# A long convolution with a soft mixture of experts: the filter's first stage kept on chip, and four moves at the end of the kernel

## The chip, the cores and the metric

The kernel runs on one core of one Trainium2 chip, everything in float32. The metric is the device time of one execution in microseconds (us). Lower is better.

## The reference, cut to what matters

```python
# x (8, 5696, 128), h (5696, 128), phi (128, 32), w1 (8, 128, 1024), w2 (8, 1024, 128)
Yf = rfft(x, n=2 * S, axis=1) * rfft(h, n=2 * S, axis=0)[None]
t = irfft(Yf, n=2 * S, axis=1)[:, :S].reshape(8 * S, 128)      # 45568 tokens
logits = t @ phi                                               # 32 slots, 4 for each of 8 experts
d = softmax of logits over the tokens (per slot)
slot_input = d.T @ t                                           # (32, 128)
slot_out[e] = relu(slot_input[e] @ w1[e]) @ w2[e]
c = softmax of logits over the slots (per token)
out = c @ slot_out                                             # (45568, 128)
```

A causal convolution of each batch with one filter h comes first. Every token then gives its logits, and all tokens together give 32 slots. The output of a token is a mixture of the 32 results, so no output can be written before the last token is through.

## The kernel before, in words

The sequence of 5696 tokens is taken as 89 rows by 64 columns, and the transform of length 5760 (N1 = 90 by N2 = 64) as matrix products in stages A, B and C. The columns are folded: column n with column 63 - n, as a sum (`comp` 0) and a difference (`comp` 1), which leaves 32 columns for each. A chunk is four columns and their four mirrors, so a batch has eight chunks. The filter h goes through the same front as the batches, as batch number 0 of nine; the 72 chunks are numbered on through them.

- Stage A. `load_x` (L178) loads a chunk. `fold` (L195) forms sum or difference on GpSimd (L200). `stage_a` (L204) multiplies the table `s1` (128x128, stationary) with 512 elements of tokens (L211), twice; ScalarE copies the two results to a tile `fst` of three buffers (L213), and two DMAs store it to `f` in DRAM (L217). TensorE handles float32 in more than one pass, so a matmul has two records in the trace.
- Stage B works on units: 23 a batch, each two of 45 rows. `load_g` (L224) loads one from `f` into a tile `gt`. `stage_b1` (L235) multiplies it (L244) in tiles of 64x64. For a batch, VectorE forms the products with the filter's spectrum, pr (L265), pi (L268) and their sum yf (L270). For the filter itself (`g == 0`), ScalarE makes `ph` (L253), VectorE from it the tiles `Hr` (L255) and `Hi` (L258), for two halves, and GpSimd the negative of Hi (L261). `stage_b2` (L274) transforms yf back (L284), ScalarE copies the result to `zst` (L288), and a DMA stores it to `z` in DRAM.
- Stage C works on pairs of chunks, 32 in all. `load_pair` (L308) loads one from `z`; c1 (L324) is the last product and the unfolding, with additions on VectorE and GpSimd (L360); c2 (L366) transposes the tokens into `yt`; c3 (L376) gives the logits `lt`; `column_max` (L386) keeps a running maximum per slot; c4 (L404) transposes the logits and takes their exponential for the dispatch; c5 (L428) transposes that one; `softmax` (L437) is the one over slots: an exponential on ScalarE (L439), the sum rs (L441), an addition (L442) and a reciprocal (L443) on VectorE, a product on GpSimd (L444); `dispatch` (L448) adds to the slots' inputs (L455, L460); c6 (L475) transposes the combine weights (L479), which go to `c_t` in DRAM, and `load_c`, `place` and `place_all` (L499, copies at L501) bring them back into the tile `cT` in the tail.

The order is written out by hand; no planner moves anything. A loop over t (L558) runs from 0 to 80. Step t holds stage A of chunk t (up to t=71), three units of stage B lagging by nine steps (LAG_B), and parts of stage C of up to six pairs lagging by 27 and more (LAG_C), interleaved by `slot_b`. From t=72 there is no stage A any more and `without_a` (L594) gives the order: even in its pairs, the steps with a c1 call `softmax` right after c5 and the additions, and the steps between hold dispatch, c2, c6, c3 and `column_max`. The last front below means these steps, t=71 to 80.

After the loop comes the tail: the last batch's pairs without stage B (from L683), `join_quarters`, the experts' two layers (hid at L801 to L812, its transposes at L819, the second layer at L827), and the slots' results `so` and `so4` (L831, L836). The output loop (from L854) multiplies 32x128 of `cT` (stationary, read in order) with `so4` (L863) into four banks per tile of up to four windows of 8 rows, copies them out on VectorE (L870) and ScalarE (L872), and stores them (L874): there every partition holds runs of four neighbouring tokens, 2 KB in DRAM.

All DMAs are issued on SyncE's queue (SP), in the order of the code, but some constants on ScalarE's. Each DMA waits until the one eight before it on its queue has landed, for its semaphore.

Of the kernel before, what the change touches and what calls it, by code (L numbers as in the profile page):

```python
# [22 lines left out]
def transform_tables(S, N1, N2, CH, X0, F0, F1):  # L23
# [11 lines left out]

    N, R1, HALF, P = N1 * N2, S // N2, N2 // 2, 2 * N2
# [8 lines left out]
    part = s1  # L45
    s1 = np.zeros((P, 3, P))
# [24 lines left out]
    return [np.ascontiguousarray(t, dtype=np.float32) for t in (s1, i1, wq, vq, tn)]  # L71
# [3 lines left out]
def kernel(  # L75
# [8 lines left out]
):  # L84

# [36 lines left out]
    t_s1, t_i1, t_w, t_v, t_turn = [  # L122
        nc.inline_tensor(t, f"tab_{n}").ap()
        for n, t in zip(("s1", "i1", "w", "v", "turn"), transform_tables(S, N1, N2, CH, X0, F0, F1))]
    fd = [nc.dram_tensor(f"f_{g}", (2, N2, NP, 2, D), F32, kind="Internal").ap() for g in range(B + 1)]
# [52 lines left out]
    def load_x(c):  # L178
# [3 lines left out]
        src = (h if g == 0 else x[g - 1]).rearrange("(a n) d -> a n d", n=N2)  # L182
# [21 lines left out]
    def stage_a(c, comp):  # L204
# [11 lines left out]
        for a, p in enumerate((F0, F1)):  # L216
            nc.sync.dma_start(  # L217
                out=fd[g][a, n0:n0 + CH, :, :, :].rearrange("n q c d -> q n (c d)"),
                in_=st[p:p + NP, :, :, :].rearrange("k n c d -> k n (c d)"))


    gs, prods = {}, {}

    def load_g(u):  # L224
        if u >= (B + 1) * NU:
# [6 lines left out]
            in_=fd[g].rearrange("a r q c d -> (a r) (q c d)")[:, 4 * i * D:(4 * i + 2 * n) * D])  # L232
        gs[u] = t_

    def stage_b1(u, adder=nc.vector):  # L235
        g, i = divmod(u, NU)
        n = min(2, NP - 2 * i)
        t_ = gs.pop(u)
# [35 lines left out]
    def stage_b2(u):  # L274
# [12 lines left out]
        st = bpool.tile([P, 2, 2 * D], F32, name="zst", tag="zst", bufs=5)  # L287
# [8 lines left out]
    ybufs = [ypool.tile([P, Q * CH, D + 1], F32, name=f"y{i}") for i in range(2)]  # L296
# [5 lines left out]
    nc.vector.memset(zring[0][:, :, :, :, :, :], 0.0)  # L302
    for t_ in (lt, dt):
        nc.vector.memset(t_[:, :, :, :], 0.0)
    for t_ in ybufs:
        nc.vector.memset(t_[:, :, D:D + 1], 1.0)
# [225 lines left out]

    def units(t):
        g, i = divmod(t - LAG_B, NJ)
        if t < LAG_B or g > B:
            return []
# [3 lines left out]
    queue = [(u, t) for t in range(steps) for u in units(t)]  # L540
# [4 lines left out]
    load_x(0)  # L545
    nc.scalar.dma_start(out=s1[:, :, :], in_=t_s1)
    for c in range(1, 3):
        load_x(c)
# [5 lines left out]
    for comp in range(2):  # L554
        fold(0, comp)
    wait_b2 = []

    for t in range(last_front + 1):  # L558
# [13 lines left out]
        def slot_b():  # L572
            fresh = bool(us)
            if fresh:
# [3 lines left out]
                wait_b2.append(u)  # L578
            if len(wait_b2) > fresh:
# [14 lines left out]
        def without_a():  # L594
# [7 lines left out]
            if T is not None:  # L602
# [10 lines left out]
                softmax(U)  # L613
# [6 lines left out]
            assert t < last_front or not (us or wait_b2)  # L620
            if t == last_front:
# [5 lines left out]
        if t == NA:  # L627
# [284 lines left out]
```

## Time and profile before

| | us |
|---|---|
| median of 3 runs | 928.26 (925.73 to 928.39) |
| profiled execution | 923.57 |
| its span in the profile | 921.4 |
| TensorE busy (PE) | 832.2, 90% of the span, 7220 instructions |
| VectorE busy (DVE) | 658.7, 71% |
| ScalarE busy (ACT) | 512.9, 56% |
| GpSimd busy (POOL) | 472.9, 51% |
| DMA | 273.04 MB, 296 GB/s on the mean |

The profile comes from one execution, whose time stands beside its span. A group line has the line of the code, the engine, the operation, the program's names of what it writes and reads, the partitions and elements, and the count; after the bar, busy time in us and mean ns of one, and after the next bar the idle time of the engine just ahead of these instructions and what ended it. A timeline line begins with its start and its duration in us; what stands in brackets at its end is the idle time before it and what ended that. A windows line gives, for a stretch of time, the busy us and the instructions of each engine, the granted TensorE clock (1.00 is full), the busy share of the DMA engines and the GB/s they moved.

The order of time is this: t=0 starts at 7.9 us, t=8 at 40.4, t=10 at 57.9, t=12 at 70.7, t=17 at 104.1, t=28 at about 200, t=71 at 681.8; the c1 steps of the last front follow each other at 19.8 us on the mean (687.6 to 786.7); the output loop runs from 855.7 to 921.4.

### The profile page before, as it was taken

The page shows a single profiled execution, that of the slowest core. Times are in us where ns is not written, and L with a number is a line of the kernel's source. Part 1 is how long each engine was busy: PE and PEld are TensorE (multiplying, and loading weights), DVE is VectorE, ACT ScalarE, POOL GpSimd, SP SyncE. Part 2 cuts the span into 40 slices and gives each one's busy share as a digit, 9 for nine tenths or more (in the row PEclk, how much of TensorE's full clock was granted, in tenths as well). Part 3 has the DMA queues.
Part 4 walks back from the last instruction along what each step waited for, and adds up shares of the span by engine and source line. Part 5 has one row for each costly group of instructions (what it writes and reads, how often), then busy time and mean ns, then how long its engine had stood idle before and what let it go on. Part 6 is the DMA issues. An engine that isn't in the chain of part 4 may idle for free. (4 is left out here: it accounts for less than half of the span.)

```text
span 921.4 us, 20366 instructions
## 1 busy us (share of the span) xinstructions
PE 832.2 (90%) x7220; PEld 401.8 (44%) x7220; DVE 658.7 (71%) x1122; ACT 512.9 (56%) x1018; POOL 472.9 (51%) x434
## 2 busy tenths in 40 slices
PE   6968888889999999999999999999997878997894
PEld 2323233334444444444444444444443334454783
DVE  3035677578888887888788888878878888685442
ACT  3546544445666565666666666656664444585442
POOL 4647632345565555555555555555544666574300
PEclk9989999999999999999999999999999998999755
DMA  9989899999999999999999999999998887783998
GB/s 294 277 264 277 268 311 332 299 290 310 307 284 314 287 305 275 324 322 299 307 341 325 290 274 316 318 292 309 312 313 259 290 276 234 256 286 138 339 405 333
DMA packets 172239, 273.04 MB, mean 296 GB/s; under 512 B 14742, under 2 KB 117398, under 8 KB 168965
## 3 DMA queue, kind: packets, MB, share of 16 engines
q1 hardware_dynamic: 171563, 271.38, 92.4%
q8 instruction: 58, 0.95, 0.4%
q10 hardware_dynamic: 576, 0.36, 0.2%
q14 instruction: 42, 0.34, 0.1%
HBM read 142.85 MB, written 128.21 MB: 294 GB/s over the span
## 5 line engine op out<-in xcount | busy, mean ns | idle before, releaser
L211 PE MATMUL bank<-x,s 128*128 128x512 f32 x576 | 284.5, 621 | 9.6 <-POOL x L200 7.9
L200 POOL TENSOR_TENSOR x<-xc 128x512 f32<-128x512 f32 x144 | 183.7, 1276 | 144.3 <-PE bank L211 90.4
L213 ACT ACTIVATE fst<-bank 128x512 f32<-128x512 f32 x288 | 167.9, 597 | 92.5 <-PE bank L211 63.5
L265 DVE TENSOR_TENSOR pr<-bt,Hr 128x512 f32<-128x512 f32 (+1 forms) x184 | 126.6, 688 | 96.7 <-PE bt L244 93.8
L288 ACT ACTIVATE zst<-bz 128x512 f32<-128x512 f32 (+1 forms) x184 | 108.2, 588 | 150.3 <-PE bz L284 140.9
L244 PE MATMUL bt<-gt,wt 64*64 64x256 f32 x1620 | 138.0, 404 | 47.9 <-DMA gt<-f 13.7
L211 PEld LDWEIGHTS bank<-x,s 128*128 128x128 f32 x576 | 100.2, 192 | 133.1 <-issue 89.5
L270 DVE TENSOR_TENSOR yf<-pr,pi 128x512 f32<-128x512 f32 (+1 forms) x169 | 145.8, 863 | 5.8
L268 DVE TENSOR_TENSOR pi<-bt,Hi 128x512 f32<-128x512 f32 (+1 forms) x184 | 125.0, 679 | 0.0
L284 PE MATMUL bz<-yf,vt 64*64 64x256 f32 x1440 | 117.2, 386 | 2.5 <-DVE yf L270 0.8
L244 PEld LDWEIGHTS bt<-gt,wt 64*64 64x64 f32 x1620 | 45.0, 132 | 164.0 <-issue 41.9
L336 PE MATMUL bank<-zc,i 128*64 128x512 f32 x448 | 108.0, 604 | 0.0
L360 POOL TENSOR_TENSOR y<-y,op 128x512 f32<-128x512 f32 x64 | 77.5, 1211 | 59.3 <-DVE op L341 56.8
L360 POOL TENSOR_TENSOR y<-y,om 128x512 f32<-128x512 f32 x59 | 81.8, 1387 | 2.1
L284 PEld LDWEIGHTS bz<-yf,vt 64*64 64x64 f32 x1440 | 52.9, 133 | 37.9 <-issue 12.8
L255 DVE SCALAR_TENSOR_TENSOR Hr<-bt,turn,ph 128x128 f32<-128x128 f32 (+1 forms) x46 | 16.0, 349 | 68.9 <-ACT ph L253 68.9
L372 ACT ACTIVATE yt<-bank 128x360 f32<-128x360 f32 x128 | 51.8, 472 | 17.0 <-PE bank L370 17.0
L370 PE MATMUL bank<-ident,y 109*128 109x109 f32 x512 | 58.1, 266 | 0.9 <-POOL y L360 0.8
L370 PEld LDWEIGHTS bank<-ident,y 109*128 109x128 f32 x512 | 49.8, 143 | 16.0 <-issue 10.8
L416 POOL MEMSET dt<- 64x8 f32 x32 | 3.4, 107 | 100.8 <-ACT dn L419 79.7
L863 PE MATMUL op<-so,cT 32*128 32x128 f32 x704 | 47.3, 398 | 5.4 <-ACT o L872 5.1
L390 DVE TENSOR_REDUCE mx<-lt 64x1 f32<-64x360 f32 x64 | 33.0, 516 | 25.0 <-ACT lt L382 24.6
(100 smaller groups left out, 895.5 us busy)
## 6 DMA issues: line engine op xcount, KB each, us to landing
f<-fst SPq DMA_DIRECT2D x288, 180.0 KB
gt<-f SPq DMA_DIRECT2D x198, 256.0 KB
z<-zst SPq DMA_DIRECT2D x176, 256.0 KB
zc<-z SPq DMA_DIRECT2D x28, 1024.0 KB
xc<-in_x_dram SPq DMA_DIRECT2D x64, 320.0 KB
out_dram<-o SPq DMA_DIRECT2D x15, 1024.0 KB
zc<-z SPq DMA_DIRECT2D x28, 416.0 KB
out_dram<-o SPq DMA_DIRECT2D x9, 768.0 KB
```

The source lines that it names most:

```text
L200: nc.gpsimd.tensor_tensor(out=y_[:, :, :], in0=t_[:, 0, :, :], in1=t_[:, 1, ::-1, :], op=AL.subtract if comp else AL.add)
L211: nc.tensor.matmul(p[:, :], s1[:, tab[G], :], src[:, :, :].rearrange("p n d -> p (n d)"), start=True, stop=True)
L213: nc.scalar.activation(st[:, :, G, :], p[:, :].rearrange("p (n d) -> p n d", d=D), AF.Copy)
L244: nc.tensor.matmul(bt[q * HP:(q + 1) * HP, a, 0:2 * D], wt[r, 2 * i + q, :], t_[r, q, :, :].rearrange("p c d -> p (c d)"), start=True, sto ...
L265: nc.vector.tensor_tensor(out=pr[r, :, :, :], in0=pv, in1=Hr[r, i, :, :].unsqueeze(2).broadcast_to([n * HP, 2, 2, D]), op=AL.mult)
L268: nc.vector.tensor_tensor(out=pi[r, :, :, :], in0=pv, in1=Hi[r, i, :, :, :], op=AL.mult)
L270: adder.tensor_tensor(out=y_[r, :, :, :], in0=pr[r, :, :, :], in1=pi[r, :, ::-1, :], op=AL.add)
L284: nc.tensor.matmul(bz[a * HP:(a + 1) * HP, q, 0:2 * D], vt[r, i, a, :], y_[r, a, :, :].rearrange("p c d -> p (c d)"), start=True, stop=True)
L288: nc.scalar.activation(st[:, 0:n, :], bz[:, 0:n, 0:2 * D], AF.Copy)
L336: nc.tensor.matmul(p[h_ * HP:(h_ + 1) * HP, :], i1[:, tab, :], t_[:, h_, o, :, q, :], start=True, stop=True)
L360: eng.tensor_tensor(out=part(v, f), in0=part(v, 0), in1=o_[:, :, :], op=sign)
L370: nc.tensor.transpose(p[:, i * TR:(i + 1) * TR], ys[T][0:TR, k * CH + i, 0:D], ident[0:TR, 0:TR])
```

## The change

1. The filter's stage A no longer goes through DRAM. `load_h` loads all of h into the space of `Hi` in runs of 8 KB; `fold_h` puts the sum into the space of `Hr` and the difference back in place. `stage_a_of_filter` takes five of the 128 feature columns at a time: the stationary operand is 89 tokens by 32 columns of the folded array for one feature (its neighbours 512 bytes apart), the moving one a new table `sh` of 90 columns, 20 matmuls into the four column tiles of one bank. Four copies put a bank's contents into four tiles that aren't used yet (zc, y, zst, yt), where stage B of the filter reads them. There are 26 such groups.
2. The order at the start. The loop begins at t=12. Before it stands stage A of the first batch's chunks 8 to 11, with seven groups of the filter after each half chunk from chunk 10 on. The filter's 23 units are spread over t=12 to 16 (before: t=9 to 16), up to two in a slot. The tiles lent to the filter are cleared on GpSimd at t=17.
3. Step t=71 has the form of `without_a`, its stage A stands at the end of step 70; in `without_a` the softmax of a pair moves to the following step, behind c2 and ahead of c6, c3 and `column_max`. The loads of the first half of w1 come two steps later.
4. In the tail, one c6 moves behind the c5 of the last chunk but one, and the last c6's move behind the transposes of the experts' hidden layer.
5. The outputs. A tile has 32 rows, 24 in the last. The stationary operand reads `cT` with a stride of four elements for 32 rows, two for 16 and none for 8, so that a partition holds 16, 8 or 4 neighbouring tokens: runs of 8, 4 or 2 KB in DRAM. Matmuls and copies are as many as before.

The diff, cut:

```diff
+    sh = np.stack([s1[:, i:i + 2].reshape(R1, 2, 2, N1 // 2).transpose(0, 2, 1, 3)
+                   for i in range(2)], 1)
...
-        t_ = gs.pop(u)
+        t_ = gs.pop(u) if g else of_filter(2 * i, n)
...
-    nc.vector.memset(zring[0][:, :, :, :, :, :], 0.0)
     for t_ in (lt, dt):
-        nc.vector.memset(t_[:, :, :, :], 0.0)
-    for t_ in ybufs:
-        nc.vector.memset(t_[:, :, D:D + 1], 1.0)
+        nc.gpsimd.memset(t_[:, :, :, :], 0.0)
+
+    def clear():
+        nc.gpsimd.memset(zring[0][:, :, :, :, :, :], 0.0)
+        for t_ in ybufs:
+            nc.gpsimd.memset(t_[:, :, D:D + 1], 1.0)
...
+    def load_h():
+        src = h.rearrange("(a n) d -> a n d", n=N2)
+        k = HALF // 2
+        for n0, gap, run in ((0, N2 - k, k), (k, HALF - k, HALF - k)):
+            for r in (slice(0, SPLIT), slice(SPLIT, R1)):
+                v, o_ = src[r, n0:n0 + run, :], hraw[r, n0:n0 + run, :]
+                v, o_ = [bass.AP(tensor=w.tensor, offset=w.offset,
+                                 ap=[w.ap[0], [gap * D, 2], [1, run * D]]) for w in (v, o_)]
+                nc.sync.dma_start(out=o_, in_=v)
+
+    def fold_h():
+        k = HALF // 2
+        for n0, eng in ((0, nc.gpsimd), (k, nc.vector)):
+            lo = hraw[:, n0:n0 + k, :]
+            up = hraw[:, N2 - 1 - n0:N2 - 1 - n0 - k:-1, :]
+            nc.vector.tensor_tensor(out=hsum[:, n0:n0 + k, :], in0=lo, in1=up, op=AL.add)
+            eng.tensor_tensor(out=lo, in0=lo, in1=up, op=AL.subtract)
+
+    HG = 5
+
+    def stage_a_of_filter(d0):
+        n = min(HG, D - d0)
+        p = bank()
+        for k in range(n):
+            for a in range(2):
+                for comp, t_ in enumerate((hsum, hraw)):
+                    r = a * HP + comp * HALF
+                    nc.tensor.matmul(p[r:r + HALF, k * 2 * NP:(k + 1) * 2 * NP],
+                                     t_[:, 0:HALF, d0 + k], sh[:, comp, a, :],
+                                     start=True, stop=True)
+        pv = p[:, 0:n * 2 * NP].rearrange("p (d c q) -> p q c d", c=2, q=NP)
+        for i, (q0, m, t_) in enumerate(homes):
+            dst, src = t_[:, :, :, d0:d0 + n], pv[:, q0:q0 + m, :, :]
+            if i in (1, 2):
+                nc.vector.tensor_copy(out=dst, in_=src)
+            else:
+                nc.scalar.activation(dst, src, AF.Copy)
...
-    load_x(0)
+    load_x(NJ)
     nc.scalar.dma_start(out=s1[:, :, :], in_=t_s1)
+    load_h()
+    nc.scalar.dma_start(out=sh, in_=t_sh.rearrange("p h a c q -> p h a (c q)"))
...
     for comp in range(2):
-        fold(0, comp)
-    wait_b2 = []
-
-    for t in range(last_front + 1):
+        fold(NJ, comp)
+    fold_h()
+    groups = list(range(0, D, HG))
+    for c in range(NJ, T0):
+        for comp in range(2):
+            stage_a(c, comp)
+            fold(c + 1, comp)
+            for _ in range(7 if c > NJ + 1 else 0):
+                if groups:
+                    stage_a_of_filter(groups.pop(0))
+        load_x(c + 3)
+    wait_b2, due = [], []
+
+    for t in range(T0, last_front + 1):
...
                 stage_b1(u)
                 wait_b2.append(u)
+                if u < NU and us:
+                    stage_b1(us.pop(0))
...
-                softmax(U)
+                due.append(U)
                 return
...
+            if due:
+                softmax(due.pop())
...
+        if t == NA - 2:
+            for comp in range(2):
+                stage_a(t + 1, comp)
...
             stage_c2(V + 1)
-            stage_c6(V - 1)
             stage_c4(V)
...
         if N == NT:
+            stage_c6(V - 1)
             stage_c4(V + 1)
...
-    for T in list(Ls):
-        stage_c6(T)
     for g in range(EG):
         for k0 in range(0, NFC, 4):
...
+    for T in list(Ls):
+        stage_c6(T)
     sop = bank()
...
+        for r0, rows in first + [(32, 32), (64, 24)]:
...
+            for at, n, r in parts:
+                for k in range(n):
+                    for q in range(Q):
+                        c = cT[q * NSL:(q + 1) * NSL, b, r:r + n * P // W, :].rearrange(
+                            "s r (j n) -> s n (r j)", n=n)
+                        nc.tensor.matmul(pq[q][:, (at + k) * D:(at + k + 1) * D], c[:, k, :],
+                                         so4[q * NSL:(q + 1) * NSL, :], start=True, stop=True)
...
+            for at, n, r in parts:
+                nc.sync.dma_start(
+                    out=ov[b, r * N2:(r + n * P // W) * N2, :].rearrange(
+                        "(p n) d -> p (n d)", p=P),
+                    in_=o_[:, at * Q:(at + n) * Q, :].rearrange("p n d -> p (n d)"))
```

## The prediction

> **What bounds the kernel now.** I read first the windows of the span, cut at the starts of the hand-written steps (a step starts at its first L211 record).
>
> ```profile
> core 0: us, PE busy (x) PEld busy (x) DVE busy (x) ACT busy (x) POOL busy (x), PEclk, DMA share, GB/s
> 8.00:40.40 32.40, 30.92 (x64) 12.03 (x64) 1.40 (x5) 16.17 (x30) 20.20 (x17) 1.00 0.95 309
> 57.90:104.10 46.20, 39.30 (x217) 14.19 (x214) 23.94 (x81) 30.05 (x68) 33.91 (x35) 1.00 0.86 254
> 104.10:201.00 96.90, 82.68 (x601) 32.03 (x599) 65.52 (x101) 46.25 (x79) 29.96 (x25) 0.98 0.97 306
> 224.00:681.00 457.00, 451.90 (x3908) 210.96 (x3904) 381.52 (x618) 281.31 (x547) 264.95 (x228) 1.00 0.98 306
> 681.00:787.00 106.00, 88.24 (x892) 40.35 (x886) 84.52 (x139) 50.59 (x101) 55.59 (x51) 0.97 0.84 270
> 787.00:855.70 68.70, 58.68 (x648) 33.38 (x644) 46.81 (x93) 41.97 (x106) 41.56 (x48) 0.98 0.69 230
> 855.70:921.40 65.70, 47.72 (x712) 45.26 (x712) 29.11 (x50) 24.69 (x50) 6.29 (x12) 0.60 0.94 361
> ```
>
> The long stretch from 224 to 681 is TensorE's: 451.9 of 457 us, at full clock. The change leaves the steps t=17..70 in the same order on every engine, so I give them nothing. It acts at the ends: t=0..7 (8.0 to 40.4, about 4 us a step, DMA at 95%); t=10..16 (57.9 to 104.1, neither TensorE nor DMA full); the last front (681 to 787, TensorE 83%); the tail (85%); the outputs (DMA 94%).
>
> Second, the timeline of ScalarE in step t=14, with two units of the filter's stage B in a row:
>
> ```profile
> 82.36 0.84 ACT L253 ACTIVATE ph<-bt,turn 128x256 f32<-128x256 f32 x2 [0.74 <-DVE Hi L258]
> 84.09 0.47 ACT L253 ACTIVATE ph<-bt,turn 128x256 f32<-128x256 f32 x1 [0.89 <-DVE Hi L258]
> 84.47 1.08 ACT L213 ACTIVATE fst<-bank 128x512 f32<-128x512 f32 x2
> ...
> 86.65 0.47 ACT L253 ACTIVATE ph<-bt,turn 128x256 f32<-128x256 f32 x1 [0.74 <-DVE Hi L258]
> ```
>
> ScalarE waits for VectorE's Hi, and VectorE for ph: they pass each unit to and fro. From 82.36 to 84.09 is 1.73 us a unit; with two fst evictions between, 84.09 to 86.65, 2.56. So a pair adds 0.83, and a step of three units and two pairs takes 6.85: 46.2/7 is 6.6, with the first step still filling.
>
> Third, timelines of ScalarE at the start, VectorE in the last front and TensorE in the tail:
>
> ```profile
> 18.54 1.08 ACT L213 ACTIVATE fst<-bank 128x512 f32<-128x512 f32 x2 [2.42 <-DMA f<-fst]
> ```
>
> ```profile
> 736.05 0.69 DVE L441 TENSOR_REDUCE rs<-L 128x16 f32<-128x512 f32 x1 [0.93 <-ACT L L439]
> 736.77 0.95 DVE L442 TENSOR_SCALAR rs<-rs 128x16 f32<-128x16 f32 x1
> 737.76 0.25 DVE L443 RECIPROCAL rs<-rs 128x16 f32<-128x16 f32 x1
> ...
> 746.25 1.05 DVE L390 TENSOR_REDUCE mx<-lt 64x1 f32<-64x360 f32 x2 [1.62 <-ACT lt L382]
> ```
>
> ```profile
> 831.47 0.81 PE L479 MATMUL bank<-ident,L 109*128 109x109 f32 x3 [2.00 <-POOL L L444]
> ```
>
> The third fst buffer comes free only when the first f store has landed, at 18.5. In the last front the softmax holds VectorE from the wait at 735.1 to 738.0, ahead of a pr, while 1.62 us stand idle later. In the tail TensorE waits 2.00 us for a softmax whose transposes (c6) are queued too early.
>
> Last, the groups by form, for what the new code is like:
>
> ```profile
> L827 PE MATMUL bank<-w2s,zd 128*32 128x128 f32 x128 | 3.7, 273 | 0.0
> L501 ACT COPY cT<-cl 128x352 f32<-128x352 f32 x8 | 6.6, 881 | 0.0
> L812 ACT ACTIVATE zd<-bank 128x512 f32<-128x512 f32 x2 | 1.2, 598 | 1.6 <-PE bank L805 1.6
> ```
>
> **What the Trainium skill says.** "SBUF — State Buffer", Specifications: SBUF lines have 16 bytes, and an access wants two hits in each or pays. That bears on the new stationary operands, whose neighbouring columns lie 512 bytes (filter) or 16 and 8 bytes (outputs) apart. The trace agrees for ScalarE's strided L501: 881 ns for 352 elements, 2.0 ns each after a start of 0.18, against 0.82 for contiguous ones (128x360 in 472 ns, 128x512 in 597). It shows no strided weight load. The page fears strides in PSUM still more; L812 reads it with 32 bytes between elements and takes 598 ns, no more than the contiguous L213, so this trace does not agree, and I price strided evictions as plain. "TensorEngine Tiling (Array Packing)", Key Properties: tiles load weights and multiply independently. The trace agrees: the four column tiles of L827 start within 20 ns of each other, a set of four records every 109 ns. "DMA: Bandwidth & Descriptors", Where 436 GB/s comes from: a ceiling of 435 GB/s. The output stores move 23.3 MB in 57.6 us, 405 GB/s, in runs of 2 KB; the large constants at the start run at 410 to 437.
>
> **The change part by part** (against the profiled execution: span 921.4, time 923.57, 2.2 around it; the median 928.26 is 1.0051 of that).
>
> *Filter up to t=12.* The old filter (8 steps of stage A, f stored and reloaded, 5.9 MB each way) goes. New: h (2.9 MB), x and constants, 7.9 MB, come ahead of the first landing of an f store, where 4.8 MB (by the DMA packets) did so by 17. At 300 to 400 GB/s 3.1 MB more take 8 to 10 us, so the wait that ended at 18.5 ends at about 27.5; two more pairs of stage A (1.98 on TensorE each, at 81.77) precede the first group: about 31. fold_h (VectorE three of 2048 columns at 1.04 ns: 6.8 us; GpSimd 4 x 1.27 = 5.1) lies in that. Then 26 groups. TensorE: 20 matmuls in two passes are 10 sets of four; a set of 90 columns by L827's rate is 109 x 90/128 = 77 ns, so 0.78 a group. Evictions go in turn ScalarE, VectorE, VectorE, ScalarE: 160 elements 0.31, 160 and 100 elements 0.50, 30 elements 0.10, and 0.12 of handing over: 1.03. Four banks let TensorE run ahead, so evictions set it: 26 x 1.03 = 26.8, and three fst pairs 3.2. t=12 starts at 31.5 + 30 = 61.5 to 62.5, before at 70.7: -8.5.
>
> The strided load is the unknown. A 32-column load takes 110 ns in L805 and L827, some 27 of which grow with columns (the skill's "TensorE: Matmul & The Clock Gate", LDWEIGHTS: columns/1.2). If only those grow 2.4-fold, 64 ns is under the set's 77: nothing. If the whole 110 does, 264 ns a set is 2.64 a group: +42. Below nothing is excluded: evictions bound the group. I take nothing, and keep +42.
>
> *t=12..16.* All 23 units lie here, up to two in a slot, where 15 were: 23 x 1.73 = 39.8 and ten fst pairs at 0.83 = 8.3, together 48 us, against 33.4 (104.1 - 70.7): +14.7, and +0.5 for the units' banks. Together with the start: **+6.8** (0 to +14 without the strided loads). gt loads, GpSimd's Hi (0.85 of 1.73) and SP's issues are under that. clear() puts 4096 columns and the y columns into GpSimd at t=17 ahead of a fold, and TensorE's stage A behind that; no large GpSimd memset is in the trace: 0 to +4, taken at 0, since the fold is needed some 4 us later and GpSimd is only 31% busy there.
>
> *Last front.* Four softmaxes move from the c1 step into the gap before mx. At most the 0.93 wait and the 1.9 of rs leave (2.8 a pair), but c1's additions on GpSimd and the exp on ScalarE stay on the same path: I take 0.9 for each of four, and 1.4 for t=71, which loses stage A's order: **-5** (-8 to +1: a softmax before mx is late by what the 1.62 doesn't cover, 0.3 to 1). The w1a loads two steps later meet SP with the same queue: 0, or +1 if a gt is behind one.
>
> *Tail.* The 2.00 goes; c4 and c5 come next at once, the moved c6 costs 0.4 of transposes: **-1.6** (-2 to +1). The last c6's after the hid transposes: 0, so's chain is VectorE's.
>
> *Outputs.* As many matmuls and evictions. Runs of 8 KB for 64 of 88 rows, 4 KB for 16, 2 KB for 8. At 425 GB/s 23.3 MB take 54.9 us, 2.7 less: **-2.5** (-5 to 0). TensorE has 178 sets at 213 ns (its clock is 0.5 here) = 38 us under 57.6 of DMA; a load slowed 2.4-fold at that clock, 511 x 178 = 91, would end +25 later unless the clock rises; I take 0.
>
> Sum: 6.8 - 5 - 1.6 - 2.5 = -2.3; span 919.1, time 921.3, and by 1.0051 **926.0**.
>
> **The rivals.** *Faster:* the filter starts earlier, because the 8 KB runs load at 430 GB/s, and units of two banks overlap better than 1.73, so that the early phase costs at most 2; last front and outputs pay 6 and 3.5. For it: between units ScalarE idles 0.74 and VectorE 0.60. Against: these are each other's. 921.4 + 1.5 - 6 - 1.6 - 3.5 = 911.8, +2.2, scaled: 918.7; with 5 off the outputs 917.
>
> *Slower:* the strided weight loads set the filter's pace: TensorE reads the column tokens slower than it multiplies, and no evictions hide it. Halfway between the bounds a group takes 2.06: 26 x 1.03 = +27, 953. It decides from 1.22 us a group on (+5 us, 931). For it: ScalarE's 2.4-fold. Against: four tiles load side by side.
>
> *Late start:* constants and h ahead of x hold f's stores, so the first group starts at 41 rather than 31: +10, 936. For it: the 2.42 wait at 18.5 for a store behind 4.8 MB. That h's transform stays off DRAM is sure by the code; that it shortens anything isn't, since stage A of the filter, DMA-bound, was only 32 us.
>
> **How the numbers follow.** Forecast 926, range of its own 919 to 933, chance 0.43; faster rival 917, 0.23; strided loads 953 (935 to 968), 0.25; late start 936, 0.09. A measurement here tells 0.3%, 2.8 us, from none: below 925.5 is faster, above 931.0 slower. Of the forecast 0.20 is faster, 0.15 the same, 0.08 slower. So faster 0.43, same 0.15, slower 0.42. Range 914 to 952: it leaves out the upper half of the strided case (0.12) and the low tail of the faster one (0.06).
>
> **What would show it.** Filter groups: start 31, period 1.03 with TensorE waiting for evictions; if TensorE has no gap and its period is over 1.2, the strided case holds. t=12 at 62, t=17 at 111. The steps t=17..70 take as long as now to 1 us. c1 to c1 in the last front 18.7 rather than 19.8. No 2.00 wait at c6. Outputs 63 us long at 420 GB/s or more, evictions waiting for DMA and not for TensorE. What would make it wrong: a group period other than 1.03, units at another period than 1.73 when two banks alternate, or a weight load in the outputs over twice as long.

## The result, and the profile after

After takes 959.6 us (median of 4 runs, 956.29 to 965.9), before 928.26 (3 runs). Runs over 1.5% above the fastest of their kernel count as slow and are left out of all medians and ratios in this document. The ratio is 1.0355, 95% interval 1.0285 to 1.0424: slower by some 33 us, where 926.0 and a range up to 952 were forecast. The profiled execution took 959.89 us, its span is 957.6, 36.2 above the one before.

First the step starts, read as before. t=12 starts at 85.0 us (before 70.7, forecast 62); t=17 at 144.6 (104.1, forecast 111); t=28 at 241.2 (201.2); t=70 at 710.3 (671.1); the outputs at 893.1 (855.7). So the difference grows by 14.3 up to t=12 and by 26.2 in t=12 to 16; then it falls by 0.5, 0.8, 1.8 and 1.2. All the loss is made in the first 145 us (one profiled execution each; how far such stretches vary is said where it matters). The windows of after, cut at these places:

```profile
core 0: us, PE busy (x) PEld busy (x) DVE busy (x) ACT busy (x) POOL busy (x), PEclk, DMA share, GB/s
...
15.20:31.20 16.00, 6.36 (x8) 2.43 (x8) 7.23 (x3) 2.39 (x4) 8.37 (x4) 0.78 0.63 169
31.20:42.50 11.30, 6.97 (x12) 2.59 (x12) 2.14 (x1) 1.81 (x4) 5.79 (x3) 0.80 0.91 328
42.50:54.00 11.50, 11.47 (x281) 11.15 (x282) 3.05 (x13) 5.73 (x16) 1.36 (x1) 0.50 0.36 104
...
65.90:85.00 19.10, 19.09 (x474) 16.06 (x473) 5.11 (x22) 13.02 (x26) 13.45 (x2) 1.00 0.13 34
85.00:109.00 24.00, 17.09 (x90) 6.24 (x89) 10.62 (x38) 12.55 (x29) 11.43 (x12) 0.79 0.37 99
109.00:144.60 35.60, 26.14 (x136) 9.44 (x132) 16.50 (x56) 19.14 (x40) 18.60 (x21) 0.80 0.40 109
...
264.20:720.00 455.80, 451.41 (x3901) 210.59 (x3897) 380.75 (x618) 281.09 (x547) 264.24 (x228) 1.00 0.98 307
721.00:826.00 105.00, 89.10 (x878) 39.22 (x876) 82.28 (x138) 49.72 (x100) 59.45 (x53) 0.95 0.84 270
826.00:895.50 69.50, 61.34 (x705) 35.46 (x703) 48.04 (x95) 43.17 (x110) 44.88 (x52) 0.97 0.69 229
895.50:957.60 62.10, 45.02 (x661) 43.64 (x658) 27.58 (x46) 23.36 (x46) 2.96 (x8) 0.71 0.93 380
```

Up to 31 us little happens but the load, and from 15.2 on DMA moves 169 GB/s. From 42.5 the filter groups run, with TensorE busy all the time, at half its clock. From 85 to 144.6, in the filter's units, no engine is full, DMA is at 0.4, and the clock is 0.8, where before it was 1.00 in t=12 to 16.

What TensorE does from 42 to 86 us is in the groups by form of that stretch:

```profile
L367 PEld LDWEIGHTS bank<-Hi,Hr 89*32 89x32 f32 x512 | 33.9, 220 | 8.5 <-ACT fst L217 7.7 <-ACT yt L376 0.8
L367 PEld LDWEIGHTS bank<-Hi 89*32 89x32 f32 x512 | 33.6, 221 | 0.0
L204 POOL TENSOR_TENSOR x<-xc 128x512 f32<-128x512 f32 x4 | 18.0, 4508 | 27.9 <-PE bank L215 22.0 <-DMA xc<-in_x_dram 5.9
L217 ACT ACTIVATE fst<-bank 128x512 f32<-128x512 f32 x10 | 12.8, 1496 | 8.8 <-DMA f<-fst 6.5 <-PE bank L215 2.3
...
L376 ACT ACTIVATE zc<-bank 128x160 f32<-128x160 f32 x25 | 9.0, 362 | 3.5 <-PE bank L367 3.3
```

A load of 32 columns takes 220 ns; L827 before took 110 for as many. And instructions that have nothing to do with the filter are stretched: the fold on GpSimd (L204) from 1.27 us to 4.51 on the mean, ScalarE's copy to fst (L217) from 0.60 to 1.50. In ScalarE's timeline it is single ones that stand still:

```profile
67.88 3.79 ACT L217 ACTIVATE fst<-bank 128x512 f32<-128x512 f32 x1 [0.25 <-PE bank L215]
...
78.34 4.37 ACT L217 ACTIVATE fst<-bank 128x512 f32<-128x512 f32 x2
```

The start, in the timelines of SyncE's queue, VectorE, GpSimd and ScalarE:

```profile
5.00 13.12 SPq L348 DMA_DIRECT2D Hi<-in_h_dram  x4
22.98 4.42 SPq L193 DMA_DIRECT2D xc<-in_x_dram  x4
...
26.22 3.85 DVE L355 TENSOR_TENSOR Hr<-Hi 89x2048 f32<-89x2048 f32 x1 [2.87 <-DMA Hi<-in_h_dram]
...
23.43 4.49 POOL L356 TENSOR_TENSOR Hi<-Hi 89x2048 f32<-89x2048 f32 x1 [7.11 <-DVE Hr L355]
28.45 6.01 POOL L204 TENSOR_TENSOR x<-xc 128x512 f32<-128x512 f32 x2 [0.52 <-DMA xc<-in_x_dram]
...
41.88 2.71 ACT L217 ACTIVATE fst<-bank 128x512 f32<-128x512 f32 x4 [6.53 <-DMA f<-fst]
```

h, 2.9 MB issued from 5.0 on, is not complete before 26.2. Its third and fourth loads are issued only at 13.4 and 17.8: they wait 7.6 and 4.1 us for the semaphores of constants that ScalarE's queue loads (`sh`, `phi`). The one eight before it, for which a DMA waits, is thus counted over both queues here, not on its own queue alone. GpSimd takes the folds of chunk 9 only behind its part of h's fold, and ScalarE waits once more for a store of f, until 41.9.

### The profile page after: what moved, and what is told of

Same layout as the page of the kernel before. It is cut to its first block, busy times and chain, and to the rows that moved or that the text cites. A ratio compares the mean times of both kernels' runs of the same rounds, so it can differ in the third digit from the quotient of the medians.

```text
span 957.6 us, 22199 instructions
## 1 busy us (share of the span) xinstructions
PE 851.4 (89%) x8180; PEld 428.1 (45%) x8180; DVE 672.5 (70%) x1169; ACT 517.8 (54%) x1038; POOL 482.4 (50%) x427
## 4 chain that ended last, share of the span: by engine, by line
PE 65%; DMA 18%; DVE 5%; ACT 4%; issue 3%; POOL 2%; SPq 1%; ACTq 0%; DVEq 0%; POOLq 0%
PE bank L215 20%; PE bank L406 11%; PE bt L249 11%; PE bz L289 7%; DMA gt<-f 5%; DMA f<-fst 5%; DMA out_dram<-o 4%; PE bank L440 3%; DMA i<-tab_i 2%; PE bank L525 2%; PE bank L367 2%; PE bank L449 2%; PE bank L501 2%; PE bank L478 1%; ACT fst L217 1%
## 5 line engine op out<-in xcount | busy, mean ns | idle before, releaser
L215 PE MATMUL bank<-x,s 128*128 128x512 f32 x512 | 265.3, 645 | 24.9 <-DMA Hi<-in_h_dram 15.2
L204 POOL TENSOR_TENSOR x<-xc 128x512 f32<-128x512 f32 x128 | 179.7, 1405 | 167.2 <-PE bank L215 106.8
L217 ACT ACTIVATE fst<-bank 128x512 f32<-128x512 f32 x256 | 158.9, 632 | 108.8 <-PE bank L215 94.9
L215 PEld LDWEIGHTS bank<-x,s 128*128 128x128 f32 x512 | 92.6, 201 | 137.0 <-issue 82.7
L249 PE MATMUL bt<-gt,wt 64*64 64x256 f32 x1440 | 122.0, 401 | 31.0 <-PE bz L289 17.4
L406 PE MATMUL bank<-zc,i 128*64 128x512 f32 x448 | 110.9, 618 | 0.0
L249 PEld LDWEIGHTS bt<-gt,wt 64*64 64x64 f32 x1440 | 39.7, 131 | 131.8 <-PE bank L215 43.6
L514 POOL TENSOR_TENSOR L<-L,rs 128x512 f32<-128x512 f32 x32 | 43.0, 1344 | 16.2 <-DVE rs L513 16.2
L406 PEld LDWEIGHTS bank<-zc,i 128*64 128x64 f32 x448 | 27.9, 139 | 50.7 <-issue 46.1
L966 PEld LDWEIGHTS op<-so,cT 32*128 32x128 f32 x704 | 45.9, 293 | 5.4 <-issue 4.1
```

The source lines that it names most:

```text
L204: nc.gpsimd.tensor_tensor(out=y_[:, :, :], in0=t_[:, 0, :, :], in1=t_[:, 1, ::-1, :], op=AL.subtract if comp else AL.add)
L215: nc.tensor.matmul(p[:, :], s1[:, tab[G], :], src[:, :, :].rearrange("p n d -> p (n d)"), start=True, stop=True)
L217: nc.scalar.activation(st[:, :, G, :], p[:, :].rearrange("p (n d) -> p n d", d=D), AF.Copy)
L249: nc.tensor.matmul(bt[q * HP:(q + 1) * HP, a, 0:2 * D], wt[r, 2 * i + q, :], t_[r, q, :, :].rearrange("p c d -> p (c d)"), start=True, sto ...
L406: nc.tensor.matmul(p[h_ * HP:(h_ + 1) * HP, :], i1[:, tab, :], t_[:, h_, o, :, q, :], start=True, stop=True)
```

## The experiments

Times are medians of three or four runs, if nothing else is said. One kernel's runs differ by up to 14 us here (`consts_ports`, 954.3 to 968.5), so small differences are read in the traces, as stretches: groups (first group to t=12) and steps (t=12 to t=17).

**The ends alone.** `ends_only`: the kernel before with the diff's parts 3, 4 and 5, without parts 1 and 2.

> The kernel before with parts 3, 4 and 5 of the change alone (last front, tail, outputs); the filter takes its old way through DRAM. If the loss lies all in parts 1 and 2, this gives the gains seen in the trace of after: tail -1.9, outputs -1.2, last front 0, so about 925 (0.996 of before). If the prediction's -5 for the last front and -2.5 for the outputs are right and hidden in after by something that parts 1 and 2 leave behind (the throttled clock, late loads), it gives about 919 (0.990). If the ends lose, 930 or more.

Measured: 923.7 us (15 runs) against 929.5 of before (16 runs) taken beside them: ratio 0.9932, interval 0.9898 to 0.9966. From t=70 to the outputs it takes 179.4 us (before 184.6), and the outputs 64.1 (65.7). It is the fastest version found, and beats both kernels. The gain is some 6 us, with an interval of 3.2 to 9.5: this does not decide between the two expectations, the 3.1 read from after's trace and the 9.1 of the prediction, though the trace, with 6.8 in the two stretches, lies between them. Parts 1 and 2 therefore cost about 36 us.

**The clock at the start.** `warm_start`:

```diff
+    def warm(n):
+        p = bps.tile([P, 2, 512], F32, name="warm", tag="bz")
+        for _ in range(n):
+            nc.tensor.matmul(p[:, 0, :], ident[:, :], lt[:, :, :, :].rearrange("p i h r -> p (i h r)"),
+                             start=True, stop=True)
...
+    warm(10)
...
+            if (c, comp) in ((NJ, 1), (NJ + 2, 0)):
+                warm(9 if c == NJ else 4)
```

> After, with idle multiplications of the identity (no reader) on TensorE while it waits at the start: 10 ahead of the first stage A, 9 behind that of chunk 8, 4 ahead of the first filter group. Theory of the clock: the groups start with the clock at 0.5 because TensorE stood idle for most of the first 42 us; kept busy, the first seven groups have a period of 1.0 instead of 1.5 and the three pairs of 31 to 38 us take 5 instead of 7: 5 to 8 us less, about 952. Theory that the strided loads set the pace whatever the clock: no gain, or up to 3 us lost to the idle work, 959 to 963.

Measured: 958.4 us. From 42.5 to 54 the clock is full, and the groups follow each other at 1.25 us instead of 1.50; the stretch is 38.8 us (after 42.5).

```profile
42.50:54.00 11.50, 11.50 (x294) 9.67 (x296) 3.46 (x14) 4.75 (x16) 0.25 (x2) 1.00 0.22 68
```

TensorE has still no gap: 1.25 us for ten sets are 125 ns a set, where I had 77. So at full clock the loads set the pace all the same. The half clock in the first groups is not a part of every execution: `warm_units`, `even`, `even_warm` and `even_fill` below have after's code up to t=12 and no idle work there, and their traces have the clock full from 33 to 36 us on and through the groups, 39.5 to 40.4 us for these, and t=12 at 78.3 to 79.1. So some 6 of after's 14.3 us up to t=12 belong to its profiled execution, about half of them to this clock, and it is no wonder that the whole hardly gains from `warm_start`. At full clock ScalarE and GpSimd are also held longer (fst 2.62 us, fold 5.34 on the mean), which may take back a part; this was not separated.

**Neighbouring columns.** `flat`:

```diff
-        "p (n d) -> p n d", d=D)
+        "p (d n) -> p n d", n=HALF)
...
-                for comp, t_ in enumerate((hsum, hraw)):
+                for comp, t_ in enumerate((hsum, hsum)):
```

> After, with the folded sum stored feature by feature, so that the 32 columns of a stationary operand are neighbours; the groups of the difference read the sum too, so the filter's difference is left out of the result, with the same number of instructions. Theory that the strided loads set the pace of the whole filter: LDWEIGHTS falls from 220 to about 110 ns and the stretch from 42.5 to 85 us falls to 27 or less: 15 to 20 us less, 940 to 944. Theory that the stride only costs where it starves other engines' access to SBUF (the evictions of 3.8 and 4.4 us at 67.9 and 78.3) and at the half clock: 6 to 10 us less, 950 to 954. Theory that late start and clock are all: 959.

Measured: 949.7 us; the stretch of the groups is 30.2 us. The same rows from 30 to 70 us:

```profile
L367 PEld LDWEIGHTS bank<-Hi,Hr 89*32 89x32 f32 x1024 | 20.0, 110 | 7.5 <-ACT fst L217 3.3 <-issue 2.3 <-ACT zc L376 1.1
...
L204 POOL TENSOR_TENSOR x<-xc 128x512 f32<-128x512 f32 x7 | 11.5, 1648 | 25.1 <-PE bank L215 19.9 <-issue 2.7 <-DMA xc<-in_x_dram 2.4
...
L217 ACT ACTIVATE fst<-bank 128x512 f32<-128x512 f32 x12 | 6.7, 595 | 16.8 <-PE bank L215 15.4 <-PE bank L367 1.4
```

The load is back at 110 ns, fst at 0.60; the folds that run beside groups take 1.28 to 1.29 each, and the stretch is what was forecast, 30. The whole is 10 us less (14 by the ratios to before, 1.0196 against 1.0355), nearer to the second expectation than to the first. So a stride of 512 bytes doubles the load and holds up ScalarE's copies to fst and GpSimd's folds meanwhile; both go with it, and in `mended` and `all_four` below, which leave nothing of the filter out, as well (0.60 and 1.28). VectorE's copies of 128x160 took 0.33 us with the stride and without: why those two were held and these were not stays open. The rest of the loss is elsewhere.

**The filter's units, t=12 to 16.** Three edits: idle work behind each unit (`warm_units`), units spread over the slots (`even`), both (`even_warm`), and both with the idle work in other banks (`even_fill`).

```diff
+        if g == 0:
+            nc.tensor.matmul(bt[:, 0, 256:512], ident[:, :],
+                             lt[:, 0:2, :, :].rearrange("p i h r -> p (i h r)"), start=True, stop=True)
```

```diff
+        slots = [3]
...
+            slots[0] -= 1
...
-                if u < NU and us:
+                if u < NU and len(us) > slots[0]:
```

In `even_fill`, `bank()[:, 0:256]` stands for `bt[:, 0, 256:512]`.

> After, with one idle multiplication of 128x256 (no reader, into an unused part of the same bank) behind each of the filter's 23 units in t=12 to 16. Theory of the clock: these steps take 59.6 us rather than the forecast 48 because TensorE, 72% busy, is granted 0.8 of its clock there, and a pair of stage A takes 3.8 to 4.9 us instead of 1.98; with 0.43 us more a unit it is over 90% busy, the clock stays full and the steps take 49 to 52: 8 to 11 us less, 949 to 952. Theory that the units' handing to and fro between ScalarE and VectorE sets these steps: no change, or 0.2 to 0.43 us more a unit, 960 to 969.

> After, with the four or five filter units of t=12 to 16 spread 2, 1, 1 or 2, 2, 1 over the three slots of a step, instead of 2, 2, 0 or 2, 2, 1. Theory: with an empty third slot the two pairs of stage A stand side by side at the end of a step, and VectorE has nothing for 3 to 4 us in each (3.71 us at 93.9 in the run with the idle work); spread, t=12 to 16 take 52 to 54 rather than 59.6: 952. Rival, the clock: TensorE stays at 0.8 and the steps at 58 or more: 957 to 960.

> After with both edits to t=12 to 16: the units spread 2, 1, 1 or 2, 2, 1, and one idle multiplication of 128x256 behind each. Alone, each took these steps from 59.6 to 56.5 and 57.1 us. If empty slot and clock are two separate causes they add: 53 to 54, and about 953. If they are one (both only fill TensorE's idle time, and so raise the clock), 56 and about 956.

> After with the units spread over the slots and one idle multiplication of 128x256 behind each unit, now into a bank of the ring of four that no unit reads, so that no engine waits for it. If the half clock and the empty slot are what t=12 to 16 lack, they take 50 to 52 us (forecast 48.6), after took 59.6: 950 to 952. If they stay at 54 or more, something in the units' chain itself is longer than the 1.73 us that were forecast.

Measured: 958.6, 957.1, 956.7 and 949.4 us; the steps 56.5, 57.1, 55.5 and 51.6 (after 59.6; 59.2 to 61.0 in the eight other experiments that leave them alone). Each edit alone gives some 3 us of the steps, and both expectations were too high. In `even_warm` they add only in part, since ScalarE has to wait for the idle work in the unit's own bank (14 times, 5.9 us together, in its trace). With that moved away, the waits are gone and the steps come to 51.6, at full clock. How much of these 8 us is the slot's and how much the clock's is not told apart: idle work in other banks alone was not run. After, and `even_fill`, in windows over these steps:

```profile
85.00:144.60 59.60, 43.23 (x221) 15.68 (x220) 27.12 (x94) 31.69 (x69) 30.02 (x32) 0.80 0.39 105
```

```profile
79.00:130.60 51.60, 45.98 (x271) 19.59 (x268) 26.98 (x94) 30.70 (x70) 29.59 (x32) 1.00 0.44 120
```

TensorE does more in 51.6 us than after in 59.6. In after's timeline the empty third slot shows as two pairs of stage A side by side, the first at half the clock (4.85 us instead of twice 1.98), and VectorE without work:

```profile
93.38 4.85 PE L215 MATMUL bank<-x,s 128*128 128x512 f32 x8
...
99.45 0.35 DVE L260 SCALAR_TENSOR_TENSOR Hr<-bt,turn,ph 128x128 f32<-128x128 f32 x1 [3.56 <-ACT ph L258]
```

**The start.** Six orders of the loads. `consts`: phi, turn and i1 on SyncE's queue. `consts_ports`: that, and h's rows on other partitions. `h_rows`: h in whole rows. `h_last`: the constants as in `consts`, chunks 9 and 10 loaded and chunk 9 folded ahead of h (chunk 10's folds stay behind h's, unlike what its expectation says). `tables_late`: wt, vt and the constants behind the stores of chunks 8 and 9. `start_both`: that, and x first, with h's fold behind that of chunk 10.

```diff
-    nc.scalar.dma_start(out=phi[:, :], in_=moe_phi)
+    nc.sync.dma_start(out=phi[:, :], in_=moe_phi)
...
```

```diff
-            for r in (slice(0, SPLIT), slice(SPLIT, R1)):
-                v, o_ = src[r, n0:n0 + run, :], hraw[r, n0:n0 + run, :]
+            for r, o in ((slice(0, HA), 0), (slice(HA, 80), HB), (slice(80, R1), HB + 80 - HA)):
+                v, o_ = src[r, n0:n0 + run, :], hraw[o:o + r.stop - r.start, n0:n0 + run, :]
...
```

```diff
...
+            nc.sync.dma_start(out=hraw[r, :, :].rearrange("p n d -> p (n d)"),
+                              in_=src[r, :, :].rearrange("p n d -> p (n d)"))
```

```diff
+    for c in range(1, 3):
+        load_x(NJ + c)
     load_h()
...
-    fold_h()
...
+            if (c, comp) == (NJ, 1):
+                fold_h()
```

```diff
         load_x(c + 3)
+        if c == NJ + 1:
+            nc.sync.dma_start(out=wt[:, :, :], in_=t_w)
+            nc.sync.dma_start(out=vt[:, :, :, :], in_=t_v)
...
```

> After, with the three small constants (phi, turn, i1) issued on SyncE's queue behind the large tables instead of on ScalarE's queue at 1.7 to 2.7 us. Theory: in after, SyncE's queue stands from 13.4 to 26.3 us because the next loads of h and x wait for semaphores of these constants, whose small packets crawl between packets of 8 and 16 KB of h. With them gone from there, the loads of x issue before 15 us, and t=12 starts 7 to 9 us earlier: about 951. Rival: the bytes of h and the tables take their time anyway, whichever queue waits: no change within 2 us of 959.

> The same move of the constants, and h's rows put on partitions 0 to 47 and 64 to 104 instead of 0 to 88 (rows 48 to 63 zero, in the table too). Theory: h loads at 213 to 233 GB/s in after [...]; spread, h takes some 8 us rather than 13: t=12 starts another 3 to 5 us earlier than with the constants alone, 947. Rival: the rate is one of the reads or of what else runs, and this is no faster than the constants alone, 951.

> After with h loaded in whole rows (32 KB a partition, two DMAs instead of four of 8 and 16 KB runs). If it is the cut into far-apart runs that holds h at 213 to 233 GB/s, h lands by 15 to 17 us instead of 23, and the first group starts at 34 rather than 38 to 42: 952 to 955. If the rate is a matter of the rows' place in DRAM or of what runs beside it, no change, and with the fold waiting for all of h up to 3 us later: 959 to 962.

> After with the loads of the chunks 9 and 10 ahead of h, their folds ahead of h's, and the small constants behind the tables on SyncE's queue. Theory: chunks 9 and 10 wait for their x behind 2.9 MB of h, and h's fold stands ahead of theirs on GpSimd, so their two pairs of stage A come just ahead of the groups; moved, they are done while h loads, and the first group starts when h is folded, at 33 to 35 instead of 38 to 42: 4 to 6 us less, 953 to 955. If the groups wait for their own data or the clock is worse, no change: 958 to 960.

> After with the two large tables (2.98 MB) and the small constants issued behind the stores of chunks 8 and 9, on SyncE's queue. Theory: the first filter group waits for ScalarE, which waits for a free fst buffer, that is for f's first store, which lies behind h and the tables at 215 to 300 GB/s; without the tables ahead of it that store lands by 30 and the first group starts when h is folded, at 33 to 35 rather than 38 to 42, and t=12 5 us earlier: 953. Rival: it is h's own rate and the half clock of the pairs ahead, and the group starts at 38 or later: 958 or more.

> After with the tables and small constants behind the stores of chunks 8 and 9, the loads of chunks 9 and 10 ahead of h, and h's fold behind the folds of chunk 10. If two holders in a row kept the first group (f's store behind the tables, the folds of chunk 9 behind h's), it now starts when h is folded: h landed at 26, folded at 33, loaded 3 us later behind x: 35 to 37 instead of 38 to 42; the gain is 3 to 5 us, 954 to 956. If it starts at 38 or later, h's own rate (2.9 MB in some 20 us) is the rest, and the order never mattered.

Measured: 956.5, 962.0, 965.5, 956.1, 957.4 and 954.1 us. The first group starts at 39.9, 43.7, 47.8, 40.3, 38.2 and, but for a first pair of matmuls that could run early, 36.9; with after's own order it started at 38.2 (`warm_units`), 38.9 (`even`) and 42.5 (after), so only `h_rows` stands clear of chance here. The theories of `consts`, `consts_ports`, `h_rows` and `tables_late` fell, `h_last` lies between its two, and `start_both` came out as expected. SyncE's queue did stand still in after, but freed (`consts`) it only queues more behind h. The partitions are not what makes h slow: its 8 KB packets took 772 ns on the mean with the rows spread, 615 in after. Nor is it the cut: 32 KB packets took 2597 ns, which for 16 engines is 202 GB/s. The last two show why one edit alone did nothing. ScalarE in `h_last`, then GpSimd in `tables_late`, then TensorE in `start_both`:

```profile
39.66 5.26 ACT L217 ACTIVATE fst<-bank 128x512 f32<-128x512 f32 x4 [17.41 <-DMA f<-fst]
```

```profile
23.05 4.49 POOL L356 TENSOR_TENSOR Hi<-Hi 89x2048 f32<-89x2048 f32 x1 [7.39 <-DVE Hr L355]
27.76 6.32 POOL L204 TENSOR_TENSOR x<-xc 128x512 f32<-128x512 f32 x2 [0.22 <-DMA xc<-in_x_dram]
```

```profile
13.99 10.70 PE L215 MATMUL bank<-x,s 128*128 128x512 f32 x20 [13.99 <-POOL x L204]
...
36.91 0.36 PE L367 MATMUL bank<-Hi 89*32 89x90 f32 x1 [2.79 <-DVE Hi L356]
```

There were two holders, one behind the other: f's store behind the tables, and chunk 9's folds behind h's. With both gone the groups start when h is folded. But then TensorE stands idle from 25 to 37 us, the clock is 0.50 from 37 to 50, and t=12 starts at 80.0, no earlier than in runs with after's order (78.3 and 78.4).

**Together.** `mended`: `consts`, `even`, and both sum and difference stored by features (the difference in two pieces, `hds`). `mended_warm`: the last two, with `warm_start` and `warm_units`. `all_four`: `tables_late`, `even_fill`, and columns by features. `all_five`: `start_both` and the other three.

```diff
+    hds = [hraw[0:R1, 8552:8552 + D1 * HALF].rearrange("p (d n) -> p d n", n=HALF),
+           hrf[:, HALF * D:HALF * (2 * D - D1)].rearrange("p (d n) -> p d n", n=HALF)]
...
+                for comp, col in enumerate((hs[:, d, :], hds[0][:, d, :] if d < D1
+                                            else hds[1][:, d - D1, :])):
```

> After with three things mended: constants moved as above, units spread as above, and the sum and the difference stored feature by feature, so that the stationary columns are neighbours (the difference in two pieces, in free parts of two tiles). If the causes add: -8 for the start, -6 for the steps, -10 for the groups, 935, still slower than the old filter way with the ends moved (923.7) since all 23 units lie in five steps. If one hides another, 941 or more.

> After with neighbouring stationary columns (sum and difference by feature), units spread, and the idle work both at the start and behind the units; the constants stay where after has them. If clock, stride and slots are together what the forecast missed in the groups and the steps, groups take 30 us, t=12 to 16 52 to 54, t=17 starts at 121 to 124, and the whole takes 938 to 942. If something else holds the steps at 55 or more, 944 or more.

> After with tables late, units spread, neighbouring stationary columns, and the idle work in other banks. If the causes add up to the miss: first group 34, t=12 at 65, t=17 at 115 to 117 (forecast 111, after 144.6), the whole 932 to 936. If they hide one another: t=17 at 122 or later, 940 or more.

> The same start, and neighbouring stationary columns, spread units, idle work in other banks. From the parts: first group 36, groups 30 to 33 us (flat 30, mended 33), t=12 to 16 51.5 (even_fill 51.6): t=17 at 118 to 121, 7 to 10 above the forecast 111, and 937 to 941 in all. If the fold of h by features, which writes with a stride, or the clock at the start eats it again: 944 or more.

Measured: 947.7, 950.8, 946.1 and 940.8 us. t=17 starts at 128.4, 134.6, 127.8 and 126.0. In all four the causes hide one another in part; `all_five` came into its range, but with t=17 5 to 8 us later than expected. In `all_five` the steps take 51.3 us, the groups 36.5 from 38.2 on: by features h's fold takes until 40.7, since its writes have a stride (4.37 and 5.08 us for a sum, `start_both` 2.29 and 4.38), and the clock is 0.63 from 37 to 50. So the causes together give back 18.6 of the 33.7 us that the forecast missed up to t=17 (144.6 - 104.1 - 6.8), some 6 of which may be after's execution alone. Of the 15 left, some 12 lie ahead of t=12 (74.7, forecast 62): the first group still waits for h, and the groups start at a lowered clock. Its ratio to before is 1.0133 (1.0038 to 1.0228): the new filter way, mended, still loses to the old one with the same ends, `ends_only`.

## Why the prediction was wrong

The steps that failed are the first two, "*Filter up to t=12.*" and "*t=12..16.*": together +6.8 forecast, +40.5 measured. The rest was small or about right. Term by term, in the order of the prediction:

- *Filter, the load*: "3.1 MB more take 8 to 10 us", first group at 31. Measured 42.5, in other runs with its order of loads 38 to 44. The rate was mis-sized: 300 to 400 GB/s were those of tables and chunks before, but h came at 213 to 231 GB/s (bytes over the mean time of a packet in after, times 16 engines), half of it was issued late, and it lay ahead of all else. VectorE's part of the fold took 9.4 us, not 6.8. Besides, I had followed SyncE's queue, but not GpSimd's, on which chunk 9's folds lie behind h's. This is the late start, which I had at 41 and gave 0.09. Why h loads so slowly stays open; its partitions and its cut were tried. Its place in DRAM alone is not it: before reads the same rows in packets of 2 KB, 117 ns on the mean up to 31 us, 279 GB/s.
- *Filter, the groups*: "evictions set it: 26 x 1.03 = 26.8". TensorE sets it: 1.25 at full clock, 1.50 at half, since "If only those grow 2.4-fold" took the milder of the two bounds. A whole load doubled, 110 to 220 ns, and a set took 125 ns, between the bounds of 77 and 264. The rival's point of decision was 1.22. The evictions as such were priced well: in after's trace a group that is not held takes 0.97 to 0.98 (72.52, 73.49, 74.47 us). The Trainium skill's "SBUF — State Buffer", Specifications, holds: far-apart columns pay, here and in the outputs (below). What I did not think of is that others pay too. The same page, SBUF: two separate sides, says that only the port shared by VectorE and GpSimd makes engines wait for each other; here ScalarE's copies took up to 3.79 us and folds up to 8.5 while TensorE loaded with a stride, and both went with the stride (`flat`). The measurement decides.
- *t=12..16*: 48 forecast, 59.6 measured. I took 1.73 a unit and 0.83 a pair from steps in which a unit stood between any two pairs, at full clock. In after the third slot is empty in steps of four units, and TensorE, 73% busy even so, gets 0.8 of its clock; with both undone the steps take 51.6. That an idle TensorE is slowed is in the Trainium skill, "TensorE: Matmul & The Clock Gate", Part 1: The HAM clock gate: half the clock after an idle window of some 3.4 us. The traces agree in part. 0.50 from 42.5 to 54 comes after idle stretches of 9.7 and 4.3 us, and with the multiplications of the identity (`warm_start`) it is 1.00 there. But the half clock lasted to 58.2 us although TensorE was busy without a gap, and in the steps of after the clock falls to a half five times, though no idle stretch of TensorE is longer than 2.7 us; in `even_fill` the longest is 1.3, and the clock stays full. There the measurement decides. I had used the clock only for the outputs, and took durations at full clock into stretches where the change itself takes TensorE's work away.
- *clear()*: 3.50 us on GpSimd at 149.2, and t=17 to 28 takes 96.6 us (before 97.1). Nothing, as taken.
- *t=17..70*: -0.5 and -0.8. As forecast, but that it fits so closely is chance: t=28 to 70, the same code in every run, took 469.2 to 478.0 us over the nineteen profiles.
- *Last front and tail*: -5 and -1.6 forecast. t=70 to the outputs takes 182.8 in after (-1.8), 179.5 to 184.1 in the sixteen experiments that share its ends (median 180.7, so -3.9), 179.4 in `ends_only`. The tail's 2.0 us are there. Of the front's 5 some 1.9 came: from c1 to c1 are 19.8 us on the mean in after and 19.3 in `ends_only` (before 19.8, forecast 18.7). After's profile shows where the rest can go. Stage A of t=71 begins 10.7 us after t=70, just as before, so what it stores is there no sooner; the first unit of the last batch, which reads it, starts 36.1 us after t=70 (before 35.9), and what was gained ahead of it turns into waiting.

The waits of TensorE, after from 710 to 826 us, and before from 671 to 787:

```profile
PE bt L249 <- PE bz L289: 9.2, 16, 0.8
PE bt L249 <- DMA gt<-f: 3.7, 1, 3.7
```

```profile
PE bt L244 <- issue: 10.2, 6, 1.8
PE bt L244 <- PE bz L284: 4.0, 9, 0.8
PE bt L244 <- DMA gt<-f: 1.7, 1, 1.7
```

The second column counts the waits, the last is the longest. 2.0 us of the gain turned into that one wait for gt.

- *Outputs*: -2.5 forecast, -1.2 in after, -1.6 in `ends_only`. The 8 KB packets take 311 ns, 421 GB/s, little under the 425 taken; those of 2 KB still 368. The strided loads there did grow, but paced nothing, since the clock was 0.71 (before 0.60), which the bound of +25 had left open. At full clock, loads of before from 856 to 860 us, with columns in order, then of after from 893 to 893.9, where they lie in order or 8 bytes apart, and from 898 to 900, where they lie 16 apart:

```profile
L863 PEld LDWEIGHTS op<-so,cT 32*128 32x128 f32 x117 | 4.2, 186 | 0.1
```

```profile
L966 PEld LDWEIGHTS op<-so,cT 32*128 32x128 f32 x32 | 1.0, 188 | 0.6 <-issue 0.6
...
L966 PEld LDWEIGHTS op<-so,cT 32*128 32x128 f32 x40 | 2.5, 324 | 0.0
```

So with two columns in each line of 16 bytes the load costs nothing more, and with one it takes 1.7 times as long: the page's rule of two hits, now with its price. At half the clock a load took 319 ns on the mean in both kernels.

Of the rivals, "*Slower:* the strided weight loads set the filter's pace" gave 953 (935 to 968), at 0.25. (Halfway between its bounds, 1.03 and 2.64, lies 1.84 a group, which is +21 and 947; 2.06 was a slip.) Its mechanism is real, but makes up about a third of the miss: without the stride (`flat`) the groups take 30.2 us, 12 less than in after and 9 to 10 less than in most other runs, of 33.7 missed (+40.5 up to t=17 instead of +6.8). That its 953 lies nearest to the 959.6 measured is luck.

## What to carry to other kernels

A duration from the profile holds at the clock and in the company in which it was taken: before it is used in a new stretch, work out how busy TensorE will be there, for a change that takes work out of a stretch can lower its clock (1.00 to 0.80 in t=12 to 16). Where an operand gets a new stride, price the milder and the harder bound, and look at who else uses SBUF at that time. Where a start is rearranged, follow every in-order queue past the moved load, the engines' own too: behind one wait that is taken away there stood a second one.

## What was not expected of the hardware

- A weight load of 32 fp32 columns 512 bytes apart: 239 to 241 ns at full clock (`warm_start`), 110 for neighbours (`flat`); of 128 columns: 324 ns when 16 bytes apart, 188 when 8 apart or in order. While the former run at full clock, a 128x512 copy on ScalarE took up to 3.8 us instead of 0.60, and an addition on GpSimd up to 8.5 instead of 1.27; ScalarE's evictions of 160 elements took 0.32 to 0.36 on the mean of a run instead of 0.32, VectorE's 0.33 as ever.
- A clock once at half stayed there for 15.7 us of work without a gap (after, 42.5 to 58.2), and for 14.8 in `start_both` (37.0 to 51.8).
- Copies from PSUM with 360 bytes between elements, written in runs of 20 bytes (zc, 128x160), took 0.31 us: no more than 0.18 and 0.82 ns an element.
- h's loads ran at 202 to 231 GB/s in packets of 8, 16 and 32 KB (after, `h_rows`), the tables at 376 to 380 in packets of 11.5 KB (after).
